# Two always-true semaphore waits on TensorE inside its matmul streams, and middle sums stored unadded, in a sort-and-sum graph kernel

## The chip, the cores and the metric

The kernel runs on one core of a Trainium2 chip. The metric is the device time of one execution in microseconds. The kernel before took 8296.54 us, the median of three executions (8286.62 to 8298.36).

## The reference

A graph has N = 10000 nodes and E = 640000 edges, with 64 channels and four components per channel. Every edge takes the features of its source node, combines them with its own four numbers `Y` through a small fixed table `cg`, scales them with a learned factor per edge and channel, and adds the result into its destination node. At the end the channels of each node are mixed.

```python
R = _silu(edge_feat @ w_rad)                                # (E, C)
xs = x[src]                                                 # (E, C, M)
tp = jnp.einsum('eci,ef,ifo->eco', xs, Y, cg)               # (E, C, M)
msg = R[:, :, None] * tp
agg = _segment_sum(msg.reshape(-1, C * M), dst, N).reshape(N, C, M)
return jnp.einsum('ncm,cd->ndm', agg, w_mix)
```

C is 64 and M is 4. The sources and destinations are random, so neither the gather nor the sum has any order to use.

## The kernel before, in words

**Sorting.** The kernel sorts the edges by destination, in DRAM, and sums them bucket by bucket. It takes the edges in three parts (`SPLIT`: 32%, 37% and 31% of them). Pass 1 sorts the edges of a part into 18 groups of 576 nodes. Pass 2 sorts a group into buckets of 32 nodes, 313 in all. A pass handles its rows in chunks of up to 12 tiles of 128 rows: VectorE spreads the payload `X` (L632) and makes one-hot matrices `oh` (L648), ScalarE makes the other one-hot matrices (L654 and L655), TensorE moves the rows to their place with one f32 matmul a tile into a PSUM tile `pr` (L662, with L664 for what carries over from the chunk before), ScalarE copies `pr` out (L669), and GpSimd stores the copy by an indirect DMA (L673).

**Messages.** The third piece of work is `messages`: 939 units, which are the 313 buckets of each of the three parts. A unit has five tiles in part 0 and six in parts 1 and 2. GpSimd gathers the source features `xg` with one indirect DMA a tile (L992). TensorE turns the edge features (L1005), ScalarE copies them (L1010), TensorE multiplies them with the radial weights (L1017, L1018), and ScalarE applies silu (L1021). VectorE makes the matrix `S` that places each edge's numbers in its node's column (L1028, L1031), and multiplies `xg` with the radial factor (L1045). TensorE then adds up the unit: one term a tile, plus sometimes one shared with the bucket before, and two f32 matmuls a term, one for each half of the channels, into one half of the PSUM tile `G` (L1058). `G` has two halves, and unit k uses half k % 2.

**Between the parts.** In part 0 ScalarE copies `G` to `Gp` (L1083), and SyncE stores it to the DRAM tile `sums`. In part 1 `fetch` reads that sum back (L1068, two units ahead, four buffers), VectorE adds it to `G` while it empties PSUM (L1081), and the sum is stored over the old one (L1085). In part 2 the same addition at L1081 goes to `Gs`. Four buckets of `Gs` are mixed with `w_mix` on TensorE (L1100) and stored as the output.

**What sets the order.** The order on each engine is written out by hand. `groups` steps pass 1 of later parts, pass 2 of the next group and the messages of the present one in turn, so a chunk's matmuls at L662 lie between the sums at L1058 of one unit and the next. Within the messages, the table `quarters` lists four quarter steps per unit, with the lead in units at which each stage runs: `(fetch, 2)` is two units ahead, and `(evict, -1)` one unit behind.

The trace shows every f32 matmul of the code as two MATMUL records, each with a weight load, so 12 tiles of a chunk are 24 records. An instruction of the built program carries one wait. Where the code needs more, the others become EVENT_SEMAPHORE instructions of their own ahead of it. The built program of before has 1270 of them on TensorE.

Of the kernel before, what the change touches and what calls it, by code (L numbers as in the profile page):

```python
# [18 lines left out]
F = mybir.dt.float32  # L19
BF = mybir.dt.bfloat16  # L20
I32 = mybir.dt.int32
OP = mybir.AluOpType
# [3 lines left out]
P = 128  # L26
B = 18
# [4 lines left out]
NB = 32  # L32
# [4 lines left out]
SPLIT = ((0.32, 5), (0.37, 6), (0.31, 6))  # L37
LG = 5
LI = 8
# [33 lines left out]
def run(gen):  # L73
    for _ in gen:
        pass


class Kernel:
    def __init__(self, ctx, tc, x, src, dst, Y, ef, w_rad, cg, w_mix, out):
        self.ctx, self.tc, self.nc = ctx, tc, tc.nc  # L80
        self.N, self.E = x.shape[0], src.shape[0]
        assert self.E % P == 0
        self.NT = self.E // P
        self.x = x.rearrange("n c i -> n (c i)")
        self.src = src.rearrange("(p t) -> p t", p=P)
        self.dst = dst.rearrange("(p t) -> p t", p=P)
        self.Y = Y.rearrange("(p t) f -> p t f", p=P)
        self.ef = ef.rearrange("(p t) f -> p t f", p=P)
        self.w_rad, self.cg, self.w_mix = w_rad, cg, w_mix
        self.out = out.rearrange("n c o -> n (c o)")  # L90
        pool = lambda n, b, **k: ctx.enter_context(tc.tile_pool(name=n, bufs=b, **k))
        self.cst = pool("cst", 1)
        self.ps = pool("ps", 1, space=bass.MemoryType.PSUM)
        self.dr = pool("dr", 1, space=bass.MemoryType.DRAM)

        N, E, T, r = self.N, self.E, 12, 14
        assert N <= 1 << 14 and BT == sum(u for _, u in SPLIT) and B % 2 == 0 and HB % 2 == 0
        self.NG = (N + GN - 1) // GN
        assert self.NG <= B
        self.part, cut = [], 0  # L100
        for i, (share, _) in enumerate(SPLIT):
            end = cut + round(self.NT * share / (2 * T)) * 2 * T if i + 1 < len(SPLIT) else self.NT
            self.part.append((cut, end))
            cut = end
        self.gt = []
        for a, z in self.part:
            nch = (z - a + T - 1) // T
            e = [min(GN, N - g * GN) * (z - a) * P / N for g in range(self.NG)]
            self.gt.append([math.ceil((m + (r - 1) / 2 * nch + 3 * math.sqrt(m + (r * r - 1) / 12 * nch)) / P)
                            for m in e])  # L110
        NG = self.NG
        self.p1 = Pass(T, r, max(map(max, self.gt)) * P // r, 6, False)
        self.p2 = Pass(12, 15, PT * P // 15, 6, True)

        self.gbase = [[(k * NG + g) * self.p1.stride + self.p1.cap - self.gt[k][g] * P // r for g in range(NG)]
                      for k in range(len(SPLIT))]
        self.NBK = (N + NB - 1) // NB
        self.pairs = (self.NBK + 1) // 2
        r = self.p2.r
        self.full = self.p2.cap  # L120
        self.most_odd = (BT * P - PT * P % r) // r
        self.least = self.full - BT * P // r

        self.btile = [0]
        for _, u in SPLIT:
            self.btile.append(self.btile[-1] + u)

        self.p1.ovf = len(SPLIT) * NG * self.p1.stride
        self.p2.ovf = self.pairs * self.p2.stride
        for q, tiles in ((self.p1, [z - a for a, z in self.part]), (self.p2, sum(self.gt, []))):  # L130
            q.none = -(-(q.ovf + sum((t + q.T - 1) // q.T for t in tiles) * P + ZR) // q.stride) * q.stride
            q.rows = q.none
        self.p1.key, self.p2.key = "grp", "bkt"
        self.xw = max(q.T * q.rw for q in (self.p1, self.p2))
        self.ot = max(q.T + q.carry for q in (self.p1, self.p2))

        self.p1.NC, self.p2.NC = 24, max(-(-t // self.p2.T) for t in sum(self.gt, []))
        self.p1.dst = self.dr.tile([self.p1.rows, self.p1.rw], F, name="grp")
        self.p2.dst = self.dr.tile([self.p2.rows, self.p2.rw], F, name="bkt")

        self.sums = self.dr.tile([self.NBK, P, 256], F, name="sums")
        self.in_group = {"grp": 0, "bkt": 0}
        self.tab = {}
        self.held, self.wanted, self.pos = None, False, None
# [427 lines left out]
    def route(self, ps, quad, nt, table):  # L572
# [4 lines left out]
        nc, wk, tc, T, Q = self.nc, self.ph, self.tc, ps.T, 2  # L577
# [80 lines left out]
        def move(c):  # L658
            X, oh, m, on = XO.pop(c)
            pr = self.ps.tile([P, 512], F, name="pr", tag="route", bufs=2)  # L660
            for u in range(m):
                nc.tensor.matmul(pr[:, :ps.rw], oh[:, u, :], X[:, u, :], start=(u == 0), stop=(not on and u == m - 1))  # L662
            if on:
                nc.tensor.matmul(pr[:, :ps.rw], oh[:, m, :], RT[c - 1], start=False, stop=True)  # L664
            PR[c] = pr
# [46 lines left out]
    def pass1(self, part, first):  # L712

        nc, ph, ps = self.nc, self.ph, self.p1
# [22 lines left out]
        def front(b):  # L737

            m = min(cut[b + 1] * T, nt) - cut[b] * T
            if b == 0 or not self.early:  # L740
                ends(b)
            if b == 0:
                for i in range(self.ahead):
                    load(i)
            if self.early:
                ends(b + 1)
            da, si = AB.pop(b), SB[b]
            yield
            key = ph.tile([P, NC * T], I32, name="key", bufs=1)
            nc.vector.tensor_scalar(key[:, :m], da[:, :m], 14, TAG, op0=OP.logical_shift_left, op1=OP.bitwise_or)  # L750
            nc.vector.tensor_tensor(si[:, :m], key[:, :m], si[:, :m], op=OP.bitwise_or)
            nc.vector.tensor_scalar(da[:, :m], da[:, :m], 1.0 / GN, 0.5 / GN - 0.5, op0=OP.mult, op1=OP.add)
            D = DB[b] = ph.tile([P, NC * T, B], BF, name="D1", bufs=2)
            yield from self.digits(ps.key, D, da, m)
            yield from self.tables(ps, D, m, self.k1, self.kov[:, 0:1], self.gb[part], self.gc[part])
            TB[b] = self.tab[ps.key]
# [145 lines left out]
    def messages(self):  # L902
# [28 lines left out]
        def index(k):  # L931
# [6 lines left out]
            key = self.pay[g][:, :n, 0].bitcast(I32)  # L938
            si = ph.tile([P, B * MT], I32, name="sidx", bufs=2)
            nc.vector.tensor_scalar(si[:, :n], key, (1 << 14) - 1, None, op0=OP.bitwise_and)  # L940
            di = ph.tile([P, B * MT], I32, name="didx", bufs=1)
            nc.vector.tensor_scalar(di[:, :n], key, 14, None, op0=OP.logical_shift_right)
            dl = ph.tile([P, B * MT], F, name="dlc", bufs=2)
            u = SPLIT[g[0]][1]
# [104 lines left out]
        def sums(k):  # L1049
            ut = tiles(k)[1]  # L1050
            G = GP[units[k]] = Gb[:, k % 2]
            V, S = VS.pop(k), SS.pop(k)
            terms = [(V[:, t], S[:, t]) for t in range(ut)]
            if k in VX:
                terms.append((VX.pop(k), SX.pop(k)))
            for t, (v, s) in enumerate(terms):
                for h in range(2):
                    nc.tensor.matmul(G[:, h].rearrange("p n f -> p (n f)"),  # L1058
                                     v[:, 32 * h:32 * h + 32, :].rearrange("p c i -> p (c i)"),
                                     s.rearrange("p n f -> p (n f)"),  # L1060
                                     start=(t + h == 0), stop=(t == len(terms) - 1), skip_group_check=True)

        def fetch(k):

            g, j = units[k]
            if g[0]:
                OLD[g, j] = ph.tile([P, 2, 4, NB], F, name="old", bufs=4)
                nc.sync.dma_start(OLD[g, j].rearrange("p h f n -> p (h f n)"), self.sums[g[1] * B + j])  # L1068

        def evict(k):  # L1070
            g, j = units[k]
# [5 lines left out]
                    GS[g, j // 4] = ph.tile([P, 2, 4, 4, NB], F, name="Gs")  # L1077
                to = GS[g, j // 4][:, :, :, j % 4, :]
            G = GP.pop((g, j)).rearrange("p h n f -> p h f n")
            if g[0]:  # L1080
                nc.vector.tensor_tensor(to, OLD.pop((g, j)), G, op=OP.add)  # L1081
            else:
                nc.scalar.activation(to, G, AF.Copy)  # L1083
            if not final:
                nc.sync.dma_start(self.sums[g[1] * B + j], to.rearrange("p h f n -> p (h f n)"))  # L1085

        def full(k):
            g, j = units[k]
# [15 lines left out]
        def mixed(k, po):  # L1104
# [4 lines left out]

        Gb = self.ps.tile([P, 2, 2, NB, 4], F, name="G", tag="G", bufs=1)  # L1110

        quarters = (((index, LI), (gather, LG), (fetch, 2), (turn, 2), (sums, 0), (silu, 1), (piece(0), 5), (piece(1), 4),
                     (piece(2), 3)), ((turned, 2), (spots, 1)),
                    ((products, 1), (evict, -1), (rest(0), 5), (rest(1), 4)), ((radial, 2), (full, -1)))
        todo, po = [], None
# [17 lines left out]
    def groups(self):  # L1133
# [23 lines left out]
        i = start = 0  # L1157
# [37 lines left out]
        while got != "ready":  # L1195
            got = next(batch) or got
        run(batch)

    def chunks(self, part):
        lo, hi = self.part[part]  # L1200
# [272 lines left out]
    def run(self):  # L1473
        tile_pool, nc = self.tc.tile_pool, self.nc
        order = [self.NG - 1] + list(range(self.NG - 1))
        self.segs = [(k, g) for k in range(len(SPLIT)) for g in order]
        with tile_pool(name="p1", bufs=2) as self.ph:
            self.rt_bufs, self.ls = 38, 8
            self.lag, self.ahead, self.early = 2, 3, 1
# [56 lines left out]
```

## Time and profile before

The profiled execution is a separate one, with the recorder on, and its time differs much from that of the timed ones.

| what | value |
|---|---|
| median of three timed executions | 8296.54 us (8286.62 to 8298.36) |
| span of the profiled execution, which is its own time as far as the page gives it | 10560.4 us |
| mean granted TensorE clock in it | 0.833 |
| TensorE matmuls busy | 7682.3 us (73%) |
| VectorE busy | 6938.2 us (66%) |
| GpSimd busy | 5869.4 us (56%) |
| ScalarE busy | 4487.3 us (42%) |

In the profile PE is TensorE's matmuls, PEld its weight loads, PEq or PEldq its sequencer, DVE is VectorE, ACT is ScalarE, POOL is GpSimd and SP is SyncE. L662 is line 662 of the kernel. An idle time is put down to what ended it. There "issue" means that the engine waited for nothing that the trace shows, and "remote" that a semaphore came whose producer the trace had already shown as done. PEclk is the granted clock as a share of full speed. The program has three uneven stretches after a prologue of about 705 us: part 0's messages to about 3842 us, part 1's to about 7264 us, and part 2's to the end.

### The profile page before, as it was taken

How to read it: one execution, taken by the hardware profiler on the slowest of the kernel's cores; microseconds unless marked ns; L12 is line 12 of the kernel's file. 1: busy time of each engine (PE TensorE's matmuls, PEld its weight loads, DVE VectorE, ACT ScalarE, POOL GpSimd, SP SyncE). 2: the span in 40 equal slices, each digit the busy share in tenths (PEclk: the TensorE clock that was granted, in tenths of full speed). 3: DMA queues.
4: the chain of work that ended last, by engine and by line, in shares of the span. 5: the costliest groups of instructions: out<-in, count | busy, mean ns of one | idle time of the engine just before them, and what ended most of it. 6: DMA issues, size and time to landing. Idle time of an engine off the chain costs nothing. (4 is left out here: it accounts for less than half of the span.)

```text
span 10560.4 us, 150281 instructions
## 1 busy us (share of the span) xinstructions
PE 7682.3 (73%) x52172; PEld 6933.0 (66%) x52172; DVE 6938.2 (66%) x13659; ACT 4487.3 (42%) x12845; POOL 5869.4 (56%) x6113
## 2 busy tenths in 40 slices
PE   8967777777777777777777777666666667676676
PEld 7857666676767666666666666655656666566665
DVE  9967777777766767667667766665555555555554
ACT  7845555555555444444434444332223223222221
POOL 2235555555556566565655665665555555555554
PEclk9978888888888878888878888887788778877878
DMA  5223333333333333333333333333233232333332
GB/s 163 88 67 92 97 90 94 93 91 96 94 94 97 92 104 106 105 111 105 110 107 104 110 109 99 112 116 102 86 95 89 87 97 86 93 90 88 94 92 79
DMA packets 688746, 1036.27 MB, mean 98 GB/s; under 512 B 270096, under 2 KB 497176, under 8 KB 687976
## 3 DMA queue, kind: packets, MB, share of 16 engines
q0 software_dynamic: 278064, 727.30, 23.8%
q1 hardware_dynamic: 407320, 291.00, 9.3%
q8 instruction: 414, 6.78, 0.3%
q10 hardware_dynamic: 2592, 8.27, 0.2%
q14 instruction: 356, 2.92, 0.1%
HBM read 836.35 MB, written 203.63 MB: 98 GB/s over the span
## 5 line engine op out<-in xcount | busy, mean ns | idle before, releaser
L992 POOL DMA_INDIRECT xg<-in_x_dram,sidx x5165 | 4931.9, 955 | 3300.8 <-issue 1343.8
L662 PE MATMUL pr<-X,oh 128*128 128x126 f32 (+1 forms) x21146 | 3178.9, 306 | 805.7 <-issue 597.7
L1058 PE MATMUL G<-S,xg 128*128 128x128 f32 x20660 | 3129.5, 313 | 816.5 <-issue 403.5
L662 PEld LDWEIGHTS pr<-X,oh 128*128 128x128 f32 x21146 | 2944.6, 215 | 1011.0 <-issue 757.1
L1058 PEld LDWEIGHTS G<-S,xg 128*128 128x128 f32 x20660 | 2920.3, 225 | 915.4 <-issue 474.5
L654 ACT ACTIVATE sq<-i,rowf 128x128 f32<-128x128 f32 x6132 | 1882.7, 391 | 1.1
L632 DVE TENSOR_TENSOR X<-dv,Wt 128x1620 f32<-128x1620 f32 (+4 forms) x906 | 1582.3, 1746 | 433.1 <-remote 211.2
L1045 DVE TENSOR_TENSOR xg<-xg,pre 128x1536 f32<-128x1536 f32 (+1 forms) x939 | 1517.4, 1616 | 524.6 <-ACT pre L1021 313.5
L1021 ACT ACTIVATE pre<-pre 128x384 f32<-128x384 f32 (+1 forms) x939 | 425.0, 453 | 1901.9 <-remote 696.3
L655 ACT ACTIVATE oh<-sq,ones 128x1024 f32<-128x1024 f32 (+3 forms) x906 | 967.2, 1068 | 26.8
L1081 DVE TENSOR_TENSOR Gs<-old,G 128x256 f32<-128x256 f32 x313 | 131.5, 421 | 1229.0 <-remote 650.4
L1031 DVE TENSOR_TENSOR S<-dv,pay 128x768 f32<-128x768 f32 (+1 forms) x939 | 836.7, 891 | 149.8 <-remote 86.4
L673 POOL DMA_INDIRECT bkt<-rt,idx x489 | 490.6, 1003 | 686.6 <-ACT rt L669 186.1
L669 ACT ACTIVATE rt<-pr 128x135 f32<-128x135 f32 (+1 forms) x906 | 242.8, 268 | 1464.0 <-remote 829.8
L673 POOL DMA_INDIRECT grp<-rt,idx x417 | 418.7, 1004 | 651.2 <-ACT rt L669 303.3
L648 DVE TENSOR_TENSOR oh<-dv,rowf 128x640 f32<-128x640 f32 (+2 forms) x869 | 717.8, 830 | 2.4 <-issue 2.2
L1010 ACT ACTIVATE sT<-pre 108x256 bf16<-108x256 f32 x939 | 354.6, 378 | 718.8 <-remote 267.5
L1100 PE MATMUL po<-wf,Gs 128*128 128x256 f32 (+2 forms) x1392 | 390.6, 442 | 193.9 <-DVE Gs L1081 176.9
L1081 DVE TENSOR_TENSOR Gp<-old,G 128x256 f32<-128x256 f32 x313 | 130.9, 418 | 568.8 <-remote 412.6
L1005 PEld LDWEIGHTS <-e 128*108 128x108 bf16 x1878 | 227.0, 141 | 410.5 <-issue 338.7
L1100 PEld LDWEIGHTS po<-wf,Gs 128*128 128x128 f32 (+2 forms) x1392 | 291.3, 215 | 275.0 <-DVE Gs L1081 183.9
L1017 PE MATMUL pre<-wr,sT 108*128 108x192 bf16 x939 | 252.7, 269 | 275.2 <-ACT sT L1010 197.7
(275 smaller groups left out, 6096.9 us busy)
## 6 DMA issues: line engine op xcount, KB each, us to landing
xg<-in_x_dram,sidx POOLq DMA_INDIRECT x5165
sums<-Gp SPq DMA_DIRECT2D x626, 128.0 KB
old<-sums SPq DMA_DIRECT2D x626, 128.0 KB
bkt<-z SPq DMA_DIRECT2D x26, 891.0 KB
pay<-bkt SPq DMA_DIRECT2D x68, 202.5 KB
ys<-in_Y_dram SPq DMA_DIRECT2D x103, 96.0 KB
es<-in_edge_feat_dram SPq DMA_DIRECT2D x103, 96.0 KB
grp<-z SPq DMA_DIRECT2D x17, 531.0 KB
```

Of the source, the lines that this page charges most:

```text
L632: nc.vector.tensor_tensor(X[:, :m, :].rearrange("p t (s w) -> p t s w", w=W), msk.unsqueeze(3).to_broadcast([P, m, ps.r, W]), QD[c // Q][1 ...
L648: nc.vector.tensor_tensor(oh[:, :v, :], self.v128.unsqueeze(1).to_broadcast([P, v, P]), row[:, o:o + v].unsqueeze(2).to_broadcast([P, v, P ...
L654: nc.scalar.activation(sq[:, u, :], self.i128, AF.Square, bias=to, scale=-1.0)
L655: nc.scalar.activation(oh[:, v:v + len(at), :], sq[:, :len(at), :], AF.Relu, bias=self.ones[:, 0:1], scale=-2.0)
L662: nc.tensor.matmul(pr[:, :ps.rw], oh[:, u, :], X[:, u, :], start=(u == 0), stop=(not on and u == m - 1))
L673: st = nc.gpsimd.indirect_dma_start(out=ps.dst, out_offset=bass.IndirectOffsetOnAxis(ap=idx[:, i:i + 1], axis=0), in_=RT.pop(c), in_offset ...
L992: nc.gpsimd.indirect_dma_start(out=xg[:, t, :], out_offset=None, in_=self.x, in_offset=bass.IndirectOffsetOnAxis(ap=si[:, u:u + 1], axis=0))
L1021: nc.scalar.activation(RT[k], RT[k], AF.Silu)
L1031: nc.vector.tensor_tensor(S[:, :ut], self.eq[:, :ut].unsqueeze(3).to_broadcast([P, ut, NB, 4]), pb[:, :, 1:5].unsqueeze(2).to_broadcast([P ...
L1045: nc.vector.tensor_tensor(V, V, R.unsqueeze(3).to_broadcast([P, ut, 64, 4]), op=OP.mult)
L1058: nc.tensor.matmul(G[:, h].rearrange("p n f -> p (n f)"), v[:, 32 * h:32 * h + 32, :].rearrange("p c i -> p (c i)"), s.rearrange("p n f -> ...
L1100: nc.tensor.matmul(po[:nn, :256], Gs[:, h, f].rearrange("p b n -> p (b n)")[:, :nn], self.wf[:, h, f, :], start=(h + f == 0), stop=(h + f ...
```

## The change

Two things change what is computed when, and one is only about buffers.

**Marks.** Two semaphores, `mark0` and `mark1`, are raised once each by TensorE itself at the start. From then on a wait for either is always satisfied. The new `mark()` issues both waits on TensorE. It is called ahead of every third tile of a chunk's products (four times in a chunk of 12 tiles) and ahead of every second term of the sums (three times in a unit of six terms). The built program of after has 7628 EVENT_SEMAPHORE instructions on TensorE where before had 1270. The matmuls and weight loads are as many as before.

**Sums unadded.** `sums` in DRAM has two slots per bucket, one for part 0 and one for part 1. Part 1 fetches nothing now: ScalarE copies `G` to `Gp` as in part 0, and SyncE stores it to the second slot. Part 2 fetches both slots in one DMA of twice the size. VectorE adds the first one to `G` and then the second one to the result, with a second instruction. `fetch` runs one unit ahead instead of two, with three buffers of double size instead of four. In the built programs VectorE's TENSOR_TENSOR instructions are 8943 in both, ScalarE's ACTIVATEs rise from 12864 to 13177, and SyncE's DMAs fall from 1879 to 1566.

**A shared buffer.** `key` and `didx`, which VectorE alone writes and reads, share one buffer.

```diff
-        self.sums = self.dr.tile([self.NBK, P, 256], F, name="sums")
+        self.sums = self.dr.tile([self.NBK, len(SPLIT) - 1, P, 256], F, name="sums")
...
             for u in range(m):
+                if u % 3 == 0:
+                    self.mark()
                 nc.tensor.matmul(pr[:, :ps.rw], oh[:, u, :], X[:, u, :], start=(u == 0), stop=(not on and u == m - 1))
...
-            key = ph.tile([P, NC * T], I32, name="key", bufs=1)
+            key = ph.tile([P, NC * T], I32, name="key", tag="key", bufs=1)
...
-            di = ph.tile([P, B * MT], I32, name="didx", bufs=1)
+            di = ph.tile([P, B * MT], I32, name="didx", tag="key", bufs=1)
...
             for t, (v, s) in enumerate(terms):
+                if t % 2 == 0:
+                    self.mark()
                 for h in range(2):
...
-            if g[0]:
-                OLD[g, j] = ph.tile([P, 2, 4, NB], F, name="old", bufs=4)
-                nc.sync.dma_start(OLD[g, j].rearrange("p h f n -> p (h f n)"), self.sums[g[1] * B + j])
+            if g[0] == FIN:
+                OLD[g, j] = ph.tile([P, FIN, 2, 4, NB], F, name="old", bufs=3)
+                nc.sync.dma_start(OLD[g, j].rearrange("p a h f n -> p a (h f n)"),
+                                  self.sums[g[1] * B + j].rearrange("a p q -> p a q"))
...
-            if g[0]:
-                nc.vector.tensor_tensor(to, OLD.pop((g, j)), G, op=OP.add)
+            if final:
+                old = OLD.pop((g, j))
+                nc.vector.tensor_tensor(to, old[:, 0], G, op=OP.add)
+                for a in range(1, FIN):
+                    nc.vector.tensor_tensor(to, to, old[:, a], op=OP.add)
             else:
                 nc.scalar.activation(to, G, AF.Copy)
-            if not final:
-                nc.sync.dma_start(self.sums[g[1] * B + j], to.rearrange("p h f n -> p (h f n)"))
+                nc.sync.dma_start(self.sums[g[1] * B + j, g[0]], to.rearrange("p h f n -> p (h f n)"))
...
-        quarters = (((index, LI), (gather, LG), (fetch, 2), (turn, 2), (sums, 0), (silu, 1), (piece(0), 5), (piece(1), 4),
+        quarters = (((index, LI), (gather, LG), (fetch, 1), (turn, 2), (sums, 0), (silu, 1), (piece(0), 5), (piece(1), 4),
...
+    def mark(self):
+        for s in self.marks:
+            self.nc.tensor.wait_ge(s, 1)
...
+        self.marks = [self.tc.alloc_semaphore("mark%d" % i) for i in range(2)]
+        for s in self.marks:
+            nc.tensor.sem_inc(s, 1)
```

On TensorE, in part 1 of the program before, a unit's sums are followed by a piece of a chunk like this. The names in brackets are the semaphores that a row waits for: DMASW those of the gathers, the others those of the engines.

```order
L1058 MATMUL G<-S,xg 128x128 [waits DMASW1_49]
L1058 MATMUL G<-S,xg 128x128
L1058 MATMUL G<-S,xg 128x128 [waits DMASW2_49]
L1058 MATMUL G<-S,xg 128x128
L1058 MATMUL G<-S,xg 128x128 [waits DMASW3_49]
L1058 MATMUL G<-S,xg 128x128
L662 MATMUL pr<-X,oh 128x126 [waits DVE_49]
L662 MATMUL pr<-X,oh 128x126 x4
L662 MATMUL pr<-X,oh 128x126 [waits Activation_49]
L662 MATMUL pr<-X,oh 128x126 x6
```

In the program after, a unit's sums and a chunk further on read as follows, with the lines moved by two to four (L1062 is L1058 of before, L664 is L662).

```order
L1062 MATMUL G<-S,xg 128x128 [waits mark1,mark0,DMASW4_49]
L1062 MATMUL G<-S,xg 128x128
L1062 MATMUL G<-S,xg 128x128 [waits DMASW5_49]
L1062 MATMUL G<-S,xg 128x128
L1062 MATMUL G<-S,xg 128x128 [waits mark1,mark0,DMASW6_49]
L1062 MATMUL G<-S,xg 128x128
...
L664 MATMUL pr<-X,oh 128x135 [waits mark1,DVE_49,mark0,Activation_49]
L664 MATMUL pr<-X,oh 128x135 x2
L664 MATMUL pr<-X,oh 128x135 [waits mark1,mark0]
L664 MATMUL pr<-X,oh 128x135 x2
L664 MATMUL pr<-X,oh 128x135 [waits mark1,mark0]
```

The two marks now stand with every third row of a chunk and every fourth of the sums (two rows are one term). The waits for other engines and for gathers stand where they stood.

On VectorE, in part 1 before, the addition at L1081 stands between the products of one unit and the chunk work that follows.

```order
L1028 TENSOR_TENSOR dv<-dv,dlc 128x192
L1031 TENSOR_TENSOR S<-dv,pay 128x768 [waits DVE_49]
L1045 TENSOR_TENSOR xg<-xg,pre 128x1536 [waits DMASW3_49,DMASW2_49,DMASW4_49,DMASW1_49,DMASW5_49,DMASW0_49,Activation_49]
L1081 TENSOR_TENSOR Gp<-old,G 128x256 [waits DMAHW7_49,DMAHW5_49,PE_49]
L983 TENSOR_TENSOR er<-pay,e_44035 128x96 [waits Activation_49]
L629 TENSOR_TENSOR dv<-dv,slot 128x180 [waits DVE_49]
```

In the program after, the same unit's products on VectorE (L1045 is L1047 there) have no such instruction behind them.

```order
L1030 TENSOR_TENSOR dv<-dv,dlc 128x192 [waits DVE_49]
L1033 TENSOR_TENSOR S<-dv,pay 128x768 [waits DVE_49]
L648 TENSOR_TENSOR oh<-dv,rowf 128x640
L1047 TENSOR_TENSOR xg<-xg,pre 128x1536 [waits DMASW3_49,DMASW2_49,DMASW4_49,DMASW1_49,DMASW5_49,DMASW0_49,Activation_49]
L985 TENSOR_TENSOR er<-er,e_51392 128x96 [waits Activation_49]
L648 TENSOR_TENSOR oh<-dv,rowf 128x640
```

The addition, with its wait for TensorE and for the fetched sum, has left VectorE in part 1. ScalarE has a row `L1091 ACTIVATE Gp<-G 128x256` for it, which waits for TensorE and for the DMA that stored the buffer's last content.

## The prediction

> **What bounds the kernel now.** I read first the spans and clocks, then the busy times by stretch, then the waits, then the lines. The busy times and clock by stretch come from the view by windows. Its columns are length, then PE, PEld, DVE, ACT and POOL busy with counts, PEclk, DMA share and GB/s.
>
> ```profile
> 0.00:705.00 705.00, 570.42 (x4183) 500.46 (x4184) 609.56 (x1440) 519.57 (x1530) 187.85 (x203) 0.91 0.34 106
> 705.00:3842.00 3137.00, 2378.69 (x16835) 2171.18 (x16835) 2263.22 (x4473) 1666.20 (x4858) 1832.02 (x1901) 0.85 0.32 94
> 3842.00:7264.00 3422.00, 2475.56 (x16970) 2253.89 (x16969) 2330.30 (x4310) 1440.98 (x4040) 2078.74 (x2166) 0.83 0.37 108
> 7264.00:10519.00 3255.00, 2253.99 (x14172) 2005.36 (x14172) 1729.59 (x3429) 860.22 (x2418) 1754.21 (x1828) 0.80 0.32 91
> ```
>
> No engine fills any message stretch. In part 1, the fullest, VectorE is busy 2330 of 3422 us (68%) and TensorE 2476 (72%). So waits make the profiled time. Those of TensorE and of its readers, from the view of waits (us in total, times, longest):
>
> ```profile
> PE pr L662 <- issue: 597.7, 788, 3.8
> PE G L1058 <- issue: 450.0, 557, 7.7
> ACT rt L669 <- remote: 829.8, 110, 14.4
> ACT pre L1021 <- remote: 696.3, 129, 19.5
> DVE Gs L1081 <- remote: 650.4, 83, 12.8
> ```
>
> Two patterns stand in these rows. TensorE pauses within its own streams with nothing to wait for ("issue"). And other engines wait up to 20 us for work that the trace shows as done ("remote"). One stretch of the timeline in part 2 shows both (start us, us, then the instruction):
>
> ```profile
> 9167.16 2.90 PE L1058 MATMUL G<-S,xg 128*128 128x128 f32 x24
> ...
> 9169.87 0.19 PEld L662 LDWEIGHTS pr<-X,oh 128*128 128x128 f32 x1
> 9170.57 0.51 PE L662 MATMUL pr<-X,oh 128*128 128x135 f32 x3 [0.51 <-issue]
> 9171.30 0.28 PE L662 MATMUL pr<-X,oh 128*128 128x135 f32 x1 [0.22 <-issue]
> ...
> 9177.70 0.58 PE L662 MATMUL pr<-X,oh 128*128 128x135 f32 x1 [1.02 <-issue]
> 9179.11 0.38 PE L662 MATMUL pr<-X,oh 128*128 128x135 f32 x1 [0.83 <-issue]
> 9180.51 2.61 PE L662 MATMUL pr<-X,oh 128*128 128x135 f32 x10 [1.02 <-issue]
> 9180.67 0.42 DVE L1081 TENSOR_TENSOR Gs<-old,G 128x256 f32<-128x256 f32 x1 [6.69 <-remote]
> ```
>
> From 9169.87 on, the chunk's matmuls come one or two at a time, 0.7 to 1.4 us apart, up to 9180.51. The last ten then run at full pace. VectorE's addition starts at 9180.67, though its sums were issued by 9170. A semaphore instruction of TensorE's sequencer stands at exactly that place, as the instructions of L1058 in this window show (its last figures are first and last start):
>
> ```profile
> L1058 PEldq EVENT_SEMAPHORE  x1: 51/51/51, 9180.6 to 9180.6; - x1
> ```
>
> So in this place one semaphore instruction goes with the end of the slow pace and with the late completion becoming visible. One place shows no cause. But the change puts such instructions every few matmuls, so this is the step on which its gain rests.
>
> **How the profile stands to the timed runs.** The profiled execution's own time is its span.
>
> ```profile
> span 10560.4 us, 150281 instructions
> ```
>
> That is 2264 us above the median of 8296.5. How much TensorE loses to slow pace follows from its two large groups and one clean chunk:
>
> ```profile
> L662 PE MATMUL pr<-X,oh 128*128 128x126 f32 (+1 forms) x21146 | 3178.9, 306 | 805.7 <-issue 597.7
> L1058 PE MATMUL G<-S,xg 128*128 128x128 f32 x20660 | 3129.5, 313 | 816.5 <-issue 403.5
> 5005.09 2.94 PE L662 MATMUL pr<-X,oh 128*128 128x135 f32 x24
> ```
>
> A clean chunk takes 2.94 us for 24, or 122 ns each. At that pace L662 needs 21146 × 0.1225 = 2590 us, and holds 3178.9 + 597.7 = 3777: 1187 too much. The sums at 2.90 / 24 = 121 ns need 2496, and hold 3129.5 + 403.5 = 3533 (with 450.0 of issue by the waits 3580): 1037 to 1084 too much. Together that is about 2250 us, cold clock included, and the profiled execution is 2264 us longer than the timed ones. The two agree too well to be passed over: nearly all of this slow pace may exist only while the recorder runs.
>
> [...]
>
> How much could be left in timed runs? A stretch of the profile that happens to be clean shows what the program can do. The window view with L1028, which starts once a unit, gives for one:
>
> ```profile
> 3241.30:3333.90 92.60, 3.86 (x12) 0.87 0.36 103
> ```
>
> Twelve units in 92.6 us are 7.72 us each. The timed median, less the prologue (705 us) and the 41 us after 10519, is 7550 us over 939 units: 8.04 each. The difference, 0.32 × 939 = 300 us, is what an end to all stalls could bring at most in a timed run. It may as well be nothing, since that stretch could be lighter than the average.
>
> **The change part by part.**
>
> *Marks, what they may bring: 0 to −300 us; I take half, −150.* For it: the observed release at 9180.6. Against it: the agreement above. There is no row between these ends to lean on, so the middle is a choice.
>
> *Marks, what they cost.* The built programs have 7628 − 1270 = 6358 more semaphore instructions on TensorE. Their price, and what one does inside a stream, is shown by the few that stand inside chunks now (all of L662's, then those of one chunk and its matmuls):
>
> ```profile
> L662 PEldq EVENT_SEMAPHORE  x293: 51/51/51, 50.5 to 7110.6; - x147
> L662 PEldq EVENT_SEMAPHORE  x1: 51/51/51, 1624.6 to 1624.6; - x1
> 1623.60 2.94 PE L662 MATMUL pr<-X,oh 128*128 128x135 f32 x24
> ```
>
> A chunk with one inside takes 2.94 us, as the one without did. So inside a stream it is hidden behind the matmuls queued ahead of it. All of them would be 6358 × 0.051 = 324 us if nothing hid them. What isn't hidden is one at the head of a stream that TensorE waited to start: 906 chunks and 939 units, 1845 × 0.051 = 94 us, of which I put a third on the path: +30 (bounds 0 and +324). The matmuls queued behind a mark wait for nothing else, since a mark is always satisfied.
>
> [...]
>
> *Sums of the middle part.* Lines of VectorE and ScalarE:
>
> ```profile
> L1081 DVE TENSOR_TENSOR Gs<-old,G 128x256 f32<-128x256 f32 x313 | 131.5, 421 | 1229.0 <-remote 650.4
> L1081 DVE TENSOR_TENSOR Gp<-old,G 128x256 f32<-128x256 f32 x313 | 130.9, 418 | 568.8 <-remote 412.6
> L1083 ACT ACTIVATE Gp<-G 128x256 f32<-128x256 f32 x313 | 119.5, 382 | 370.8 <-remote 162.2 <-PE G L1058 154.4 <-issue 14.9
> L983 DVE TENSOR_TENSOR er<-pay,e 128x80 f32<-128x80 f32 (+3 forms) x261 | 61.5, 236 | 0.8 <-issue 0.8
> ```
>
> In part 1 VectorE loses 313 × 418 = 131 us and ScalarE gains 313 × 382 = 120. ScalarE has 1441 of 3422 us busy there, so it hides them, unless its in-order queue is held: behind a copy that waits for late sums stand the silu and the chunk copies, and TensorE and VectorE wait for those. VectorE's in-order queue is freed of the same wait (568.8 us idle ahead of that line). In part 2 VectorE gains a second addition. No such SBUF addition of 256 is in the trace; it lies between 236 ns (80 elements) and 421 (256 from PSUM), so 74 to 132 us, and I take 421. It follows the first without a wait, and `G` is free after the first, so TensorE isn't held longer. VectorE is busy 1730 of 3255 us there (53%), which hides it. If that cover is gone in timed runs, it costs 132. Of the 131 in part 1 I credit somewhat over a third, because VectorE is at 68% there and not at 100%: −50 (bounds −131 and +130).
>
> *Fetch.* It falls from two units to one ahead, about 8 us in a timed run, for 256 KB instead of 128; part 1's 313 fetches go, 41 MB. No wait at L1081 is put down to this transfer now, in any of 626, so I cost it at nothing. If it came late by 1 us a unit in part 2, that would be +313, and SyncE's queue would show it. The shared buffer lies within VectorE's order: nothing.
>
> *Sum.* 8296.5 − 150 + 30 − 50 = 8126.5, so 8127 us. Against the profiled execution the same step is larger: of 10560 it would take away up to 2250 us of slow pace, and I expect a span below 10000.
>
> **The rivals.**
>
> 1. *The stalls are the recorder's, and the marks do nothing in a timed run.* They are hidden as in the chunk at 1624.6, and the sums alone count: 8296.5 − 50 = 8247 us, 0.6% faster, with a profile that may be much shorter all the same. For it: 2250 against 2264 us. Against it: 8.04 against 7.72 us a unit. Chance 0.25.
> 2. *Nothing can be measured* (within 0.2%, 17 us, about what a measurement of this kernel can tell from no change; the three runs spread over 12 us). The marks do nothing, and VectorE's 131 us in part 1 come back as 74 to 132 in part 2: about 8296. That is the rival in which the change doesn't do what it says, since the work only moves. Chance 0.13.
> 3. *Slower: the marks' sequencer time lands on the path.* With no slow pace in timed runs TensorE's queue runs empty at each chunk and unit, and a mark ahead of three matmuls delays them. With half of 324 us on the path and the sums at −50: 8296.5 + 162 − 50 = 8409 us, 1.4% slower. It decides once more than about a fifth of the marks is unhidden while they cure nothing ((50 + 17) / 324 = 0.21). Against it: 2.94 us with and without. For it: only one semaphore instruction stood in that chunk, where now several do. Chance 0.20.
>
> The forecast itself, stalls partly there and partly cured, has 0.42.
>
> **How the numbers follow.** Faster by over 0.2%: the forecast and rival 1, 0.42 + 0.25 = 0.67. Same: 0.13. Slower: 0.20. The range reaches up to 8380, which leaves out the worse part of rival 3 (some 0.1). Down it reaches to 8296.5 − 300 − 131 = 7866, rounded to 7860, which leaves out some 0.08. The forecast's own range is 7860 to 8240.
>
> **What would show it.** In the profile after, the issue waits of the two matmul lines (597.7 and 450.0) should fall to under a half, and the remote waits of L669, L1021 and L1081 with them; TensorE's own 122 ns inside a clean chunk should stay. The addition should be gone from VectorE in part 1, with a second one in part 2. If the span falls far and the timed median by less than 1%, rival 1 holds. If chunks of 24 take visibly over 2.94 us, rival 3 holds. The forecast is wrong if the waits stay as they are, or if L1081's waits are then put down to the fetch.

## The result, and the profile after

The changed kernel takes 8346.05 us (8343.38 to 8351.61, four runs), against 8297.45 us before: the ratio is 1.006, with a 95% interval of 1.0045 to 1.0074. It is slower by 49 us, where the prediction said 8127 and faster.

The profiled execution after has a span of 8343.9 us, as long as its timed runs. The stages of after come from the view by windows, cut where the first unit of each part starts (columns as in the prediction):

```profile
0.00:714.00 714.00, 560.67 (x4184) 489.65 (x4185) 608.24 (x1440) 521.07 (x1531) 188.31 (x203) 0.94 0.34 105
714.00:3209.00 2495.00, 2108.43 (x16742) 1966.04 (x16742) 2249.57 (x4458) 1644.21 (x4822) 1816.87 (x1884) 0.92 0.41 117
3209.00:5926.00 2717.00, 2165.16 (x17006) 2035.46 (x17005) 2219.80 (x4001) 1528.52 (x4372) 2062.46 (x2148) 0.89 0.42 121
5926.00:8286.00 2360.00, 1949.65 (x14167) 1771.71 (x14168) 1851.93 (x3746) 877.59 (x2433) 1792.34 (x1863) 0.91 0.51 144
```

Beside the profile of before, this looks like a gain of 2200 us. It isn't one. The kernel before was profiled a second time (the run `e8_before_again` below), and the same stages of that execution read:

```profile
0.00:681.00 681.00, 557.96 (x4185) 487.18 (x4185) 608.75 (x1441) 522.76 (x1535) 187.24 (x203) 0.94 0.35 110
681.00:3172.00 2491.00, 2101.53 (x16737) 1961.22 (x16738) 2248.45 (x4457) 1644.02 (x4816) 1813.78 (x1885) 0.92 0.41 118
3172.00:5885.00 2713.00, 2196.57 (x17008) 2051.92 (x17007) 2320.64 (x4310) 1447.36 (x4061) 2058.79 (x2148) 0.89 0.47 136
5885.00:8233.00 2348.00, 1944.17 (x14164) 1772.59 (x14164) 1717.92 (x3438) 871.82 (x2431) 1781.01 (x1862) 0.91 0.45 127
```

Its span is 8287.8 us. So the profiled execution of before that the prediction read (10560.4 us) was a disturbed one, and comparisons of traces below take the second. From the result on, the profiled execution is itself one of the timed ones (that of after took 8345.70 us), so being profiled doesn't by itself make this kernel slow. Between the two undisturbed traces the change costs 33 us before the first unit, 4 in part 0, 4 in part 1, 12 in part 2 and 3 behind it, 56 in all.

The waits of TensorE after (us in total, times, longest) show where the 33 us are:

```profile
PE pre L1007 <- DVE xg L1047: 457.5, 226, 7.3
PE po L1107 <- DVE Gs L1089: 165.9, 41, 7.1
PE G L1062 <- ACT Gp L1091: 144.6, 75, 17.0
PE pr L664 <- DVE oh L648: 139.1, 90, 8.4
PE pre L1019 <- ACT sT L1012: 86.4, 62, 5.4
PE cnt L384 <- issue: 59.5, 1, 59.5
```

The last row is one single wait of 59.5 us, put down to "issue", at L384. The long issue rows of the prediction are gone from this view. The timeline of TensorE's first matmuls shows that this wait is the start of the program:

```profile
59.46 1.62 PE L384 MATMUL cnt<-D,sel 128*64 128x216 bf16 x8 [59.46 <-issue]
62.89 0.37 PE L406 MATMUL prep<-R,U 8*64 8x18 f32 x2 [1.81 <-ACT Wt L779]
```

In the second profile of before, the same matmul runs at 14.88 us, and waits for VectorE:

```profile
14.88 1.60 PE L384 MATMUL cnt<-D,sel 128*64 128x216 bf16 x8 [14.88 <-DVE D L357]
26.48 0.36 PE L406 MATMUL prep<-R,U 8*64 8x18 f32 x2 [10.00 <-ACT Wt L777]
```

What TensorE does in these 59.5 us is shown by the instructions of the marks' line (L1208) in that window, and then in the next one up to 705 us (last figures: first and last start):

```profile
L1208 PEldq EVENT_SEMAPHORE  x536: 51/51/51, 1.1 to 59.4; - x179
L1208 PEldq EVENT_SEMAPHORE  x59: 51/51/51, 601.7 to 700.5; - x59
```

536 semaphore instructions stand in a row ahead of the first matmul, (59.4 − 1.1) / 535 = 109 ns apart. In the trace each of them waits for both semaphores, so that one instruction is one call of `mark()`. (The sentence ahead of the prediction, that an instruction carries one wait, holds for the matmuls and weight loads, of which none in the trace has more than one, and not for these: 4048 of TensorE's semaphore instructions have two.) 536 marks are 134 chunks of four: those of the first pass of part 0 (32% of the edges are 133.3 times 12 tiles of 128 rows). In that stretch TensorE's order isn't written out by hand, a scheduler sets it, and a wait for a semaphore that is already raised depends on nothing there. In the hand-ordered stretch the marks stand where they were written, 5771 of them from 705.2 to 8297.4 us. The profile names none of this as a wait, since a sequencer's semaphore instructions don't count as busy: it says "issue".

Not all of the delay reaches the units. The first matmul is 59.46 − 14.88 = 44.6 us later, but the next one shown (L406) had waited 10.00 us for ScalarE and now waits 1.81, so 8 us are taken up there.

### The profile page after: what moved, and what is told of

It reads as the page before. It is cut to its first block, busy times and chain, and to the rows that moved or that the text cites. A ratio compares the mean times of both kernels' runs of the same rounds, so it can differ in the third digit from the quotient of the medians.

```text
span 8343.9 us, 156785 instructions
## 1 busy us (share of the span) xinstructions
PE 6799.7 (81%) x52172; PEld 6275.9 (75%) x52172; DVE 6939.8 (83%) x13659; ACT 4572.2 (55%) x13158; POOL 5877.5 (70%) x6113
## 5 line engine op out<-in xcount | busy, mean ns | idle before, releaser
L1062 PE MATMUL G<-S,xg 128*128 128x128 f32 x20660 | 2806.9, 297 | 171.3 <-ACT Gp L1091 144.6
L664 PE MATMUL pr<-X,oh 128*128 128x126 f32 (+1 forms) x21146 | 2730.1, 287 | 265.0 <-DVE oh L648 139.1
L664 PEld LDWEIGHTS pr<-X,oh 128*128 128x128 f32 x21146 | 2611.6, 199 | 334.1 <-DVE oh L648 120.6
L1062 PEld LDWEIGHTS G<-S,xg 128*128 128x128 f32 x20660 | 2658.3, 210 | 208.8 <-ACT Gp L1091 169.3
L1047 DVE TENSOR_TENSOR xg<-xg,pre 128x1536 f32<-128x1536 f32 (+1 forms) x939 | 1516.7, 1615 | 618.6 <-DMA xg<-in_x_dram,sidx 337.8
L1091 ACT ACTIVATE Gp<-G 128x256 f32<-128x256 f32 x626 | 238.9, 382 | 826.8 <-PE G L1062 579.8
L1007 PE MATMUL pre<-identb,e 128*108 128x128 bf16 x1878 | 274.8, 229 | 458.7 <-DVE xg L1047 457.5
L975 ACT ACTIVATE e<-er 128x240 bf16<-128x240 f32 (+6 forms) x522 | 205.1, 393 | 303.9 <-DVE er L985 284.5
```

The lines of the kernel that those rows point to most:

```text
L1007: nc.tensor.matmul(pre[:KR, 256 + 128 * h:384 + 128 * h], e[:, 36 * t:36 * t + KR], self.identb, start=True, stop=True)
L1047: nc.vector.tensor_tensor(V, V, R.unsqueeze(3).to_broadcast([P, ut, 64, 4]), op=OP.mult)
L1062: nc.tensor.matmul(G[:, h].rearrange("p n f -> p (n f)"), v[:, 32 * h:32 * h + 32, :].rearrange("p c i -> p (c i)"), s.rearrange("p n f -> ...
```

## The experiments

Theory A was that the marks cost what was lost, and theory B that the unadded sums do. The first four runs were to tell these apart.

**The marks alone** (`e1`; the kernel before with the diff's `mark()` and its two calls).

> The kernel before with the marks alone. Theory A (the marks' 6358 semaphore instructions of 51 ns cost what was lost; the sums come out even): about 8350 us, ratio 1.005 to 1.008. Theory B (the marks are free in a timed execution, the unadded sums cost the 49 us): 8297 us within 15. Theory C (both matter, with opposite signs): the marks at 8380 or above, or below 8280. In all of them, if the slow pace is the recorder's and the marks end it, the profiled span falls from 10560 to within 20 us of the timed median.

It took 8327.92 us against 8292.93: 1.0043 (1.0029 to 1.0057), +35 us. Theory A, then, for most of it. The profiled span is 8324.5.

**The unadded sums alone** (`e2`; the change without `mark()`).

```diff
             for u in range(m):
-                if u % 3 == 0:
-                    self.mark()
...
-                if t % 2 == 0:
-                    self.mark()
```

> The change without the marks: middle sums unadded, fetch one unit ahead. Theory A: 8297 us within 20, or faster. Theory B: about 8346 us, ratio 1.005 to 1.007. Theory C: away from both, so that its difference to before and that of the marks alone sum to +49. If the marks are what keeps the recorder from slowing the kernel, the profiled span is again far above the timed median, over 10000 us.

It took 8300.79 us: 1.0011 (1.0002 to 1.0020), +8 us. With the marks' 35 this makes 43 of the 49; the other 6 lie within the intervals. Its profiled span is 8297.4 us, though it has no marks. So the expectation on the recorder fell: marks aren't what makes a profile undisturbed.

**Marks ahead of every tile and every term** (`e3`; against the marks alone).

```diff
-                if u % 3 == 0:
+                if True:
...
-                if t % 2 == 0:
+                if True:
```

> The kernel before with marks ahead of every tile and every term, about 12 in a chunk for 4 and 6 in a unit for 3. Theory A: about two and a half times the cost of the marks alone, some +125 us, 8420 us. Theory B: still 8297 us within 20, unless the sequencer itself becomes TensorE's limit (a mark pair of 102 ns a tile beside 245 ns for a tile's two matmuls leaves it below that).

It took 8445.0 us: 1.0185 (1.0171 to 1.0199), +152 us, 4.3 times the cost of the marks alone instead of two and a half times. That the size was off led to the answer. In the first 176 us of this kernel the marks' line (L1205) holds three times the 536, which is 134 chunks of twelve marks:

```profile
L1205 PEldq EVENT_SEMAPHORE  x1608: 51/51/51, 1.1 to 175.8; - x179
```

TensorE's first matmul is late by 175.8 − 14.9 = 161 us, and the kernel is 152 us longer. With 536 it is late by 44.6, and 33 to 36 us longer.

**The middle part's copy on VectorE** (`e4`; with the marks).

```diff
-                nc.scalar.activation(to, G, AF.Copy)
+                if g[0]:
+                    nc.vector.tensor_copy(to, G)
+                else:
+                    nc.scalar.activation(to, G, AF.Copy)
```

> The change with the middle part's copy out of PSUM on VectorE instead of ScalarE, so that ScalarE's work and its in-order queue are those of before, and VectorE has in part 1 the instruction of before without its fetch. Theory A: 8346 us or up to 100 us slower (VectorE keeps its 131 us in part 1 and has 131 more in part 2). Theory B, if ScalarE's held queue is the cost: 8300 us or below; if the second addition is the cost: 8346 us or above.

It took 8338.19 us: 1.0058 (1.0044 to 1.0071), which the change's 1.006 can't be told from. Where the copy runs makes no difference of a size that this shows, so ScalarE's held queue (8300 us or below) is not the cost.

Theory D came from the starts above: only the marks that were moved to the program's start cost time. The next two runs split the marks by place.

**Marks only in the hand-ordered stretch** (`e5`; against the marks alone).

```diff
     def mark(self):
-        for s in self.marks:
+        for s in self.marks if self.ordered else ():
             self.nc.tensor.wait_ge(s, 1)
...
+        self.ordered = True
         with tile_pool(name="p2", bufs=2) as self.ph:
```

> The kernel before with the marks only in the stretch whose order is written out by hand, none in the first pass of part 0, where a scheduler sets the order. Theory D (536 marks of that first pass, which depend on nothing, were all moved to the program's start, where TensorE works them off in 59.5 us before its first matmul; the others are hidden): 8293 us within 15, first matmul at 15 us. Theory A as first put (the cost is spread over the 6358 marks): 8293 + 32 = 8325 us or little less, since over 90% of the marks are still there.

It took 8289.64 us against 8288.95: 0.9999 (0.9990 to 1.0008). The trace has 5830 marks, over 90% of those in the change, and they cost nothing that can be measured:

```profile
L1205 PEldq EVENT_SEMAPHORE  x5830: 51/51/51, 566.8 to 8244.3; - x195
```

**Marks only in the first pass of part 0** (`e6`; the same edit with `if not self.ordered`).

> The kernel before with the marks only in the first pass of part 0, all others left out. Theory D: as long as the marks alone, 8325 us (+30 to +40), first matmul at 59 us. Theory A as first put: 8293 + 3, less than a tenth of the cost.

It took 8324.27 us: 1.0041 (1.0027 to 1.0054), +35 us. 536 marks give all that 6366 gave. Their trace:

```profile
L1205 PEldq EVENT_SEMAPHORE  x536: 51/51/51, 1.1 to 59.3; - x179
```

Theory D holds on both sides, and theory A in its first form (a cost spread over the marks) is out.

**The copy on VectorE without marks** (`e7`; `e2`'s kernel with `e4`'s edit).

> Without marks: middle sums unadded, but copied out of PSUM by VectorE. The unadded sums alone measured +8 us. If ScalarE's held queue is their cost: 8293 us within 5. If the second addition in part 2 is the cost: 8300 us or above, since VectorE keeps 131 us in part 1 and has 131 more in part 2. If VectorE bounded part 1 at all, this should be longer than the unadded sums alone by up to 131 us; if it bounds neither part, all three are within 10 us of each other.

It took 8299.43 us: 1.0013 (1.0004 to 1.0022), +10 us, against +8 with the copy on ScalarE. VectorE has 131 us more work in part 1 than in `e2`, and 131 more in part 2 than before, and the time shows 2 us of the first and 10 of the second. So VectorE's work bounds neither part.

**The kernel before, profiled again** (`e8_before_again`).

> The kernel before itself, for a second profiled execution. If the slow pace belongs to this program whenever the recorder is on, the span is again near 10560 us. If it belonged to that one execution, the span is near 8295 us, and no mark was needed to end it.

The span is 8287.8 us, of an execution that was timed at 8289.58. All thirteen profiles after the first one agree with their timed runs in this way, with marks or without. The runs of the experiments were on three chips. The record doesn't name the chip of the disturbed execution, so the place isn't ruled out.

If VectorE doesn't bound part 1, something else does. In the second profile of before, the timeline of GpSimd in part 1 reads (last, the idle time before the instruction):

```profile
4404.12 0.96 POOL L992 DMA_INDIRECT xg<-in_x_dram,sidx  x1 [0.30 <-issue]
4405.39 0.94 POOL L992 DMA_INDIRECT xg<-in_x_dram,sidx  x1 [0.30 <-issue]
4406.63 0.95 POOL L992 DMA_INDIRECT xg<-in_x_dram,sidx  x1 [0.30 <-issue]
4407.88 0.95 POOL L992 DMA_INDIRECT xg<-in_x_dram,sidx  x1 [0.30 <-issue]
4409.14 0.94 POOL L992 DMA_INDIRECT xg<-in_x_dram,sidx  x1 [0.30 <-issue]
4410.38 1.00 POOL L673 DMA_INDIRECT grp<-rt,idx  x1 [0.30 <-ACT oh L655]
```

Every instruction has the same gap of 0.30 us ahead of it, whatever the view puts it down to. In all of part 1 the trace has no gap under 0.303 or over 0.315 us, so it is read here as the price of issuing one and not as idle time. The windows of that profile give 2148 GpSimd instructions in part 1's 2713 us: 1.263 us each, which leaves nothing between them. Part 2 is the same, with 1862 instructions in 2348 us, gaps of 0.303 to 0.315 us and 1.261 us each. In part 0 some 100 us are left over. Theory G is that GpSimd bounds part 1. The last runs tested it by doses.

**More gathers in part 1** (`e9` and `e10`). One gather more in every third unit, and then in every unit:

```diff
+            if g[0] == 1 and j % 3 == 0:
+                xd = ph.tile([P, 256], F, name="xd", bufs=1)
+                nc.gpsimd.indirect_dma_start(
+                    out=xd, out_offset=None, in_=self.x,
+                    in_offset=bass.IndirectOffsetOnAxis(ap=si[:, u:u + 1], axis=0))
```

> The kernel before with one gather more in every third unit of part 1 (105 in all, into a buffer that nobody reads; key and didx share a buffer, for room). Theory G (GpSimd bounds part 1: its 2148 DMA instructions take 2713 us, 1.26 us each, busy time and issue gap together): +105 x 1.26 = +132 us. Rival V (VectorE bounds part 1): +0 to +20 us.

> The same in every unit of part 1, 313 gathers more. Theory G: +313 x 1.26 = +394 us, three times the run before. Rival V: at most +100 us.

They took 8500.38 us, 1.0242 (1.0228 to 1.0256), and 8913.08 us, 1.0741 (1.0727 to 1.0756), against 8299.20: +201 and +614 us. The two are in proportion to the counts (3.05 for 2.98), but each gather costs 1.92 to 1.96 us instead of 1.26. The rows of the added line, of the third and of the whole dose, say why:

```profile
L997 POOL DMA_INDIRECT xd<-in_x_dram,sidx x105 | 100.4, 956 | 100.8 <-DMA xd<-in_x_dram,sidx 72.2 <-issue 14.3 <-DVE st L453 2.4
```

```profile
L997 POOL DMA_INDIRECT xd<-in_x_dram,sidx x313 | 299.5, 957 | 317.0 <-DMA xd<-in_x_dram,sidx 227.4 <-issue 54.5 <-DVE oh L648 4.4
```

With a single buffer `xd`, some of the added gathers wait for the one before to land, which the expectation had not counted. Busy and idle time of the added line together are 201.2 and 616.5 us, and the kernel grew by 201 and 614. Whatever GpSimd does longer in part 1, by work or by waiting, the kernel takes longer. Part 1 alone grew: in the whole dose from 2713 to 3328 us, by 615, in the windows of that run.

```profile
3164.00:6492.00 3328.00, 2261.25 (x17002) 2111.82 (x17000) 2324.35 (x4311) 1448.76 (x4061) 2358.85 (x2465) 0.82 0.43 123
```

**More work for VectorE in part 1** (`e11`; the first instruction of `S`, L1028, twice).

```diff
+            for _ in range(2 if g[0] == 1 else 1):
-            nc.vector.tensor_tensor(self.eq[:, :ut], self.i32.unsqueeze(1).to_broadcast([P, ut, NB]),
+                nc.vector.tensor_tensor(self.eq[:, :ut], self.i32.unsqueeze(1).to_broadcast([P, ut, NB]),
```

> The kernel before with the first instruction of S computed twice in part 1, 313 times 0.36 us = 113 us more of VectorE. Theory G: +0 to +25 us. Rival V: +90 to +113 us.

It took 8299.35 us against 8299.20: 1.0002 (0.9992 to 1.0011). VectorE is busy 2432 us in part 1 for 2321, and part 1 is as long as before:

```profile
3171.00:5885.00 2714.00, 2204.93 (x16996) 2055.82 (x16996) 2431.97 (x4623) 1448.12 (x4061) 2059.32 (x2149) 0.90 0.47 136
```

111 us more of VectorE cost nothing, as the 313 additions fewer in `e2` and in the change brought nothing.

**One addition in part 2 only** (`e12`; against the unadded sums alone).

```diff
                 nc.vector.tensor_tensor(to, old[:, 0], G, op=OP.add)
-                for a in range(1, FIN):
-                    nc.vector.tensor_tensor(to, to, old[:, a], op=OP.add)
```

> Without marks: middle sums unadded, fetched as in the change (both slots, one unit ahead), but the second addition of part 2 is left out, and with it part 1's share of the sums. If the second addition is what makes part 2 some 11 us longer in the unadded sums alone: 8290 us, as before, within 5. If the later or larger fetch is: 8300 us still.

It took 8301.73 us against 8299.20: 1.0001 (0.9992 to 1.0010). The expectation's 8290 and 8300 us were set against a before of some 8289 us, so here the ratio counts. The interval of the unadded sums alone (1.0002 to 1.0020) overlaps with it, so the times don't settle whether the second addition makes the few microseconds.

The traces say more. In part 2 of the second profile of before and of after, shown by the windows above, GpSimd has 1862 and 1863 instructions, and no gap over 0.32 us, but it is busy 1781.0 and 1792.3 us. These 11 us are the 12 by which part 2 is longer. Over all runs, GpSimd's busy time in part 2 is 1777 to 1785 us in the eight with one addition and the fetch of before, 1788 to 1794 in the four with two additions and the change's fetch, and 1784 in this one, with one addition and the change's fetch. So the second addition makes most of it, in single profiles a few microseconds apart. It reaches the time not because VectorE is full, but because GpSimd's gathers take 959 ns on average there instead of 953, as the lines of part 2 alone show, first in the second profile of before, then after. Why they do is not shown.

```profile
L992 POOL DMA_INDIRECT xg<-in_x_dram,sidx x1710 | 1629.7, 953 | 521.0 <-issue 466.1 <-DMA xg<-in_x_dram,sidx 13.1 <-PE G L1058 8.2
```

```profile
L994 POOL DMA_INDIRECT xg<-in_x_dram,sidx x1711 | 1640.6, 959 | 521.6 <-issue 469.2 <-DMA xg<-in_x_dram,sidx 14.6 <-DVE Gs L1087 9.5
```

## Why the prediction was wrong, point by point

**"The marks, −150 us".** This step failed, and with it the sign: the marks in the hand-ordered stretch, where the stalls had been seen, brought nothing (`e5`, 0.9999). It rested on stalls that belonged to one disturbed execution, whose granted clock was 0.833 where the second one's was 0.909. The prediction saw that its 2250 us of slow pace nearly equalled the 2264 us between profile and timed runs, and still credited half of the remaining 300 us. The release that spoke for the marks doesn't stand either: in the prediction's own rows the matmuls run again at 9180.51, and the semaphore instruction comes at 9180.6. Nor is what follows full pace: the last ten start (9182.70 − 9180.51) / 9 = 0.24 us apart, where the clean chunk's take 0.122 each. In the second profile of before the stalls aren't there: L662 waits for VectorE most (first row below), and all of its issue time, weight loads with it, is 47.0 us:

```profile
  DVE oh L648: 320.0, 191
...
  issue: 47.0, 72
```

The 7.72 us a unit of one clean stretch was no measure of what could be had either. Undisturbed, the units take 2491 / 313 = 7.96 us in part 0, 8.67 in part 1 and 7.50 in part 2. The stretch lies in part 0, whose units have five tiles, and was set against the mean of all three parts. What stays open is the cause of the disturbed execution. Marks aren't needed to end the slow pace, since kernels without them (`e2`, `e7`, `e8`) were profiled undisturbed too. Nor is the recorder enough for it: it was on in the thirteen others as well, and the span of `e8` is 8287.8 us of a timed 8289.58. That it slowed the one execution isn't shown.

**"The marks' cost, +30 us".** The size was right (+35), and that is luck, since the place and the working weren't. The third of 1845 marks at the heads of streams cost nothing (`e5`). 536 marks that were moved to the program's start cost all of it. The prediction took the order of the hand-ordered stretch for the order everywhere. The price was off too: a mark's record lasts 51 ns, but marks in a row come 109 ns apart, so the row's duration isn't what one takes. Hence 536 × 0.109 = 58 us, of which the first 14.9 lie beside the wait for VectorE that was there anyway, and 8 more are taken up at L406. Each of these instructions waits for two semaphores. Whether the 109 ns are the price of one instruction or of two semaphores at 55 each, no run here separates.

**"Hidden inside a stream".** Right: 2.94 us with a semaphore instruction as without, and about the same with two. Two chunks of after, the first with one mark within its time and the second with two (its matmuls are wider):

```profile
4218.70 2.84 PE L664 MATMUL pr<-X,oh 128*128 128x126 f32 x24
4238.47 2.95 PE L664 MATMUL pr<-X,oh 128*128 128x135 f32 x24
```

**"The unadded sums, −50 us".** Wrong in sign, by a small amount: +8 us alone. VectorE lost its 313 additions in part 1, and is busy 2220 us there for 2321, but the time came back as a wait. The lines of VectorE in part 1 alone show it at the products, first in the second profile of before, then after (L1047 is L1045 there; idle time before it and what ended it stand last):

```profile
L1045 DVE TENSOR_TENSOR xg<-xg,pre 128x1536 f32<-128x1536 f32 x313 | 546.9, 1747 | 105.7 <-ACT pre L1021 53.3 <-DMA xg<-in_x_dram,sidx 41.1 <-issue 4.9
```

```profile
L1047 DVE TENSOR_TENSOR xg<-xg,pre 128x1536 f32<-128x1536 f32 x313 | 547.3, 1748 | 268.7 <-ACT pre L1023 119.0 <-DMA xg<-in_x_dram,sidx 110.3 <-DMA bkt<-rt,idx 17.4
```

VectorE waits 163 us longer there, for gathers and for ScalarE's silu, and part 1 didn't get shorter, since GpSimd sets its length. The two additions in part 2 read:

```profile
L1089 DVE TENSOR_TENSOR Gs<-Gs,old 128x256 f32<-128x256 f32 x313 | 133.5, 427 | 10.7
L1087 DVE TENSOR_TENSOR Gs<-old,G 128x256 f32<-128x256 f32 x313 | 129.9, 415 | 146.7 <-PE G L1062 146.2
```

427 ns for an addition from SBUF is above the upper bound of 421 that was worked with. Of these 133 us, part 2 shows 12 as longer time, by way of GpSimd (`e12`). No wait of the additions is put down to the fetch, as was said.

**"No engine fills any message stretch."** Here the first mistake lies, and the page of before had the row to see it (its largest group):

```profile
L992 POOL DMA_INDIRECT xg<-in_x_dram,sidx x5165 | 4931.9, 955 | 3300.8 <-issue 1343.8
```

The 1343.8 us of issue stand ahead of 4354 of the gathers, 0.31 us each. That is the fixed gap. The row of part 1 in the prediction gives the sum: 2166 GpSimd instructions, busy 2078.7 us, with 0.30 us ahead of each are 2729 us. That is all of the 2713 us which part 1 takes undisturbed (with 2148 instructions in its window there), but against the 3422 of the disturbed profile it looked like idle time. So GpSimd fills part 1, and a change that spares VectorE could bring nothing there.

**The rivals.** Rival 1 (the stalls are the recorder's) came nearest to what happened to the stalls, and its 8247 us failed on the sums and on the start. Its sign, a span that falls far while the timed runs hardly move, came true, but the second profile of before shows the same fall without any change, so the sign could tell nothing. Nor are the stalls the recorder's as such, since fourteen executions were profiled and one had them. Rival 3 (slower) had the right sign and 63 us too much; its mechanism, marks unhidden on the path, held in one place only. That 8346 lies within the range, below 8380, is owed to the room left for rival 3. The range's lower half and the 0.67 for faster hung on a profile that its own time contradicted.

## What to carry to other kernels

When a profiled execution is a quarter longer than the timed runs, take a second one before reading its waits as the kernel's; here the 2264 us that it had too much weren't there to be gained. An instruction that depends on nothing stays where it was written only if the order is fixed there: look for it at the program's start in every stretch that a scheduler orders, where 536 marks stood here. And count an engine's fixed gap per instruction as its work: GpSimd, busy 76% of part 1 with 0.303 to 0.315 us ahead of each instruction, had no time to spare there.

## What the runs showed of the hardware

- A semaphore instruction on TensorE that waits for two semaphores, both satisfied, is recorded with 51 ns, but 536 and 1608 in a row took 58 and 175 us, 109 ns each. Between matmuls, 5830 semaphore instructions with one or two such waits cost nothing measurable (0.9999, 0.9990 to 1.0008).
- One of the profiled executions of this kernel ran TensorE's streams at 0.7 to 1.4 us a step for stretches and had other engines wait up to 19.5 us for work that the trace shows as done, at a mean granted clock of 0.833 and 10560 us. The other execution of the same kernel had 0.909 and 8288 us.
- GpSimd's indirect gather of 128 rows takes 0.95 us, and in parts 1 and 2 of the second profile of before every GpSimd instruction had a gap of 0.303 to 0.315 us ahead of it. A dose of 313 gathers appeared in the kernel's time to within 3 us of their busy and idle time (614 against 616.5).
- With a second 128x256 f32 addition a unit on VectorE in part 2, GpSimd's gathers there took 959 ns in place of 953, and part 2 was 12 us longer. With that addition left out they took 955.
